# Three more chunks whose activations come already turned round, normalised by GpSimd

## The chip, the cores and the metric

The kernel runs on one core of a Trainium2 chip. A core has five engines that run side by side and meet only at semaphores: TensorE (PE in the profile; its weight loads are PEld), VectorE (DVE), ScalarE (ACT), GpSimd (POOL) and SyncE (SP), which here does nothing but start DMA transfers. ACT and POOL also start some. The transfers of all queues share 16 DMA engines. Each engine executes its instructions in the order in which the program lists them, so an instruction that waits holds up all that stand behind it on that engine or queue.

The metric is device time in microseconds (us) for one execution: 358.87 before the change, the median of three runs (358.83 to 359.21).

## The reference

Two branches work on the same normalised rows, and their results are added to the input. S = 2048 rows, D = 448, F = 1792, all float32.

```python
x  = A_q
xn = _layernorm(x)                      # over the 448 columns, no weights
# A: short convolution of k (4 taps), times v, a long causal convolution by FFT, gate
k_shift = sum(k_pad[:, t:t + S] * shift_k[:, ks - 1 - t] for t in range(ks))
kv = k_shift * v
y  = causal_conv(kv, ssm_k) + kv * ssm_D
# B: dense 448 -> 1792, Mish, dense 1792 -> 448
h  = einsum("bsd,df->bsf", xn, w1) + b1
B  = einsum("bsf,fd->bsd", mish(h), w2)
return x + xn * y + B
```

## The kernel before, in words

**Tiling.** The 2048 rows lie as 128 partitions by 16 tiles; two tiles make a chunk of 256 rows, so there are 8 chunks, c = 0 to 7. The dense branch handles one (chunk, pair of 128-wide blocks of F) after another: 8 chunks by 7 pairs, 56 pairs. Pair i takes two slots of the schedule: in slot 2i the first product `g1_mm(i)` (22 matmuls, line 512), in slot 2i+1 the Mish of that pair on ACT (`mish`, line 520, then a split by lines 84 and 85) and the second product `g2_mm(i-2)` of the pair two before (12 matmuls, lines 544 to 546). To keep float32 precision at the fast matmul rate every operand is split into a high part (a rounding copy on ACT) and a low part (a subtraction on DVE): `XH`/`XL` for the activations, `w1h`/`w1l`, `w2h`/`w2l` for the weights, `ach`/`acl` for the Mish results. In g1_mm of a pair of chunk 1 or later the first seven matmuls need only XH; then come four that need XL.

**The long convolution** is an FFT by matmuls, threaded through the same slots. In slots 6 to 59 it transforms 8 groups of the filter (`h`) and 8 of kv: load, `f1_mm` (line 146, 8 matmuls), `f1_fold` (a copy on ACT, line 152, and two DVE operations, line 156, into one of two buffers `st`), and `f1_out`, which stores st to device memory (line 167), from the POOL queue for the two filter groups in slots 6 and 9, from ACT's afterwards. kv is made by `taps` on DVE (lines 189 to 202) and one tap on POOL (`taps_pool`, line 182), for which `skb`, the four rows of shift coefficients repeated on 128 partitions, must be there.

**The order** is written by hand: `at(slot, ...)` puts work ahead of the slot's products, `after(slot, ...)` behind them; within a slot the order is that of the calls. The loop over chunks stands last, so its loads are the last of their slot. Some DVE work is put in a list (`drip`), of which one item is issued at each call `dv()`, that is, behind most DVE operations; a flush empties the list.

**Weights.** During chunk 0 the raw weights arrive pair by pair on SP's queue (w1, w2 in turn) and are split once: `w2_load(4)` in slot 9, `w2_load(5)` in slot 10, `w2_split(4)` at the end of slot 11, `w2_split(5)` at the end of slot 13.

**Normalising, two ways.** The first product needs the activations with D on the partitions. `NT = 4` is the first chunk that uses the second way.

- Chunks 1 to 3 (`ln_stats`, `ln_T`): q is loaded with rows on the partitions; DVE takes mean and variance (lines 406, 409, 412), POOL the power -1/2 (415), subtracts and multiplies (419), copies a tail (423); in the last two slots before the chunk, eight PE transposes (line 464, two sets of four) turn the result, and ACT and DVE split it out of PSUM (476, 474). The transposes need `ident`, a part of the tile `con`.
- Chunks 4 to 7 (`nt_...`): q is loaded the same way for the statistics, and a second copy, already turned by the host, goes to the tile `xn` (`xT_load`, line 434, 512 KB; there is one buffer xn). Mean and factor are stored to device memory (`nt_store`, POOL's queue, line 442, 2 KB) and read back as a row repeated on all partitions (`nt_row`, SP's queue, line 445, 128 KB, one for each half of the chunk) into `idr`, which lies over `ident`. DVE subtracts and multiplies by that row (`nt_norm`, line 451, two operations of 128x512 for a half), ACT and DVE split (`nt_split`, 458, 459).

The slots of the second way are counted from a base b = 14(c-1), plus 1 where the table says so:

```python
NT_AT = {"q": -5, "x": -1, "stats": -2, "flush": 0, "row": (4, 8), "norm": (7, 10), "split": (8, 11)}
```

Of the kernel before, what the change touches and what calls it, by code (L numbers as in the profile page):

```python
# [17 lines left out]
NP = NF // 2  # L18
CH = 256
NCHUNK = S // CH  # L20
NO = 8
EPS = 1e-5

G2_LAG = 2
# [5 lines left out]
I2_AT = {100: ((6, 7, 0, 1), 92, (95, 97, 98, 99), (0, 2, 0, 1)),  # L30
         108: ((2, 3, 4, 5), 101, (104, 105, 106, 107), (0, 1, 0, 1))}
LATE = 2
NT = 4
NT_AT = {"q": -5, "x": -1, "stats": -2, "flush": 0, "row": (4, 8), "norm": (7, 10), "split": (8, 11)}
NT_SOON = dict(NT_AT, row=(4, 5), norm=(4, 7), split=(6, 8))
NT_HOW = {c: NT_SOON for c in (3, 4, 7)}
NT_HOW[5] = dict(NT_AT, q=-8, stats=-4, flush=-2)
WARM_N = (448, 448, 448)
FILL_N = (224, 112, 96)
# [3 lines left out]
def tile_kernel(ctx: ExitStack, tc, q, qT, k, v, sk, hT, sD, w10, w1, w2, c_fib, c_g, c_gi, c_i2, out):  # L43
    nc = tc.nc
    V = nc.vector
# [17 lines left out]
    Dkv = dp.tile([NO * 16, 32, D], F32, name="Dkv")  # L63
    E = dp.tile([NJ * 4, 64, D], F32, name="E")
    MR = {c: dp.tile([2, CH], F32, name="MR") for c in range(NT, NCHUNK)}

    con = cp.tile([128, 64 + CH], F32, name="con")
    f1, ident, idr = con[:, 0:64], con[:, 64:192], con[:, 64:]
# [6 lines left out]
    def rs(c):  # L75
        return rstd[:, 2 * c:2 * c + 2] if c < NT else mv[:, 2 * c:2 * c + 2, 1]

# [26 lines left out]
    def dv(n=1):  # L104
        for _ in range(n):
            if drip:
                drip.pop(0)()
# [4 lines left out]
    def at(slot, fn, *args):  # L112
        plan.setdefault(int(slot), []).append((fn, args))

    def after(slot, fn, *args):
        plan2.setdefault(int(slot), []).append((fn, args))
# [4 lines left out]
    skb = sp1.tile([128, 4, D], F32, name="skb")  # L121
# [273 lines left out]
    def xn_tile():  # L395
        return mp.tile([128, 4, CH], F32, name="xn", bufs=1)

    def ln_parts(c):
        st = mp.tile([128, 2, 6], F32, name="bst", bufs=2)
        ve = mp.tile([128, 2], F32, name="ve", bufs=2)  # L400
        if c < NT:
            XN[c] = xn = xn_tile().rearrange("p a b -> p (a b)").rearrange("p (j d) -> p j d", j=2)
        eng = nc.gpsimd if 0 < c < NCHUNK - 1 else V

        def stats(jj):
            V.bn_stats(st[:, jj], Q[c][:, jj])

        def aggr(jj):
            V.bn_aggr(mv[:, 2 * c + jj], st[:, jj])

        def eps(a, b):
            V.tensor_scalar(ve[:, a:b], mv[:, 2 * c + a:2 * c + b, 1], EPS, None, op0=ALU.add)  # L412

        def power(a, b):
            nc.gpsimd.tensor_tensor(rs(c)[:, a:b], ve[:, a:b], mhalf[:, a:b], op=ALU.pow)  # L415

        def norm(jj):
            j = 2 * c + jj
            eng.tensor_scalar(xn[:, jj, :D], Q[c][:, jj], mv[:, j, 0:1], rs(c)[:, jj:jj + 1],
                              op0=ALU.subtract, op1=ALU.mult)  # L420

        def tail(a, b, copy=eng.tensor_copy):
            copy(xn[:, a:b, D:], xn[:, a:b, D - 64:D])

        return stats, aggr, eps, power, norm, tail, ve
# [15 lines left out]
    def nt_store(c):  # L441
        nc.gpsimd.dma_start(MR[c].rearrange("j (p t) -> p j t", t=2), mv[:, 2 * c:2 * c + 2])

    def nt_row(c, jj):
        nc.sync.dma_start(idr, MR[c][jj].partition_broadcast(128))

    def nt_norm(c, jj):
        x = XN[c][:, :, 128 * jj:128 * jj + 128]
        for t, op in enumerate((ALU.subtract, ALU.mult)):
            m = idr.rearrange("p (a t) -> p t a", t=2)[:, t:t + 1].to_broadcast([128, 4, 128])  # L450
            V.tensor_tensor(x, x, m, op=op)
            dv()

    def nt_split(c, jj):
        if jj == 0:
# [22 lines left out]
    def ln_T(c, jj):  # L478
        if jj == 0:
            dv(len(drip))  # L480
            x_tiles(c)
        p = pg()
        transposes(c, jj, p)
        for lo in range(2):
            x_split(c, jj, p, lo)
# [73 lines left out]
    def mlp_slot(s):  # L559
# [3 lines left out]
        if half == 0:  # L563
            if i < n:
                c, p = pairs[i]
                if c + 1 < NT:
                    if p == 0:
# [8 lines left out]
        else:  # L576
            if i < n:
                c, p = pairs[i]
                if p == NP - 2 and c + 1 < NT:
                    ln_T(c + 1, 0)  # L580
# [21 lines left out]
        after(t, f1_fold, g, "h")  # L602
        at(t + (2 if t < 12 else 3), f1_out, Dh, g, "h", nc.gpsimd if t < 12 else nc.scalar)

    at(12, lambda: nc.sync.dma_start(skb, sk.partition_broadcast(128)))
    for g in range(-2, 0):
        at(12, k_load, g)
    for g, t in enumerate(KV_AT):
        d = t - (KV_AT[g - 1] if g else t - 6)
        at(t - d - (3 if g > 1 else 2), k_load, g)  # L610
        at(t - d - 1, v_load, g)
        for u in range(4):
            after(t - (2 if g else 1) - d + d * u / 4, taps, g, u)
        at(t, f1_mm, KV, g, "kv")
        if g + 1 < NO:
            after(t, taps_pool, g + 1, 2)
        after(t, f1_fold, g, "kv")
        at(t + (3 if g < NO - 1 else 2), f1_out, Dkv, g, "kv")

    for p in range(NP):  # L620
        if p >= 3:
            at(max(2 * p - 5, 0), w1_load, p)
        if p == 1 or p > 2:
            at(2 * p - 2, w1_split, p)
        p and at(2 * p + (1 if p < 5 else 0), w2_load, p)
        at(2, w2_split, p) if p == 0 else after(2 * (p + G2_LAG) - 1, w2_split, p)

    at(OCT_AT[0], regroup)
    for o in range(NO):
# [34 lines left out]

    for c in range(NT, NCHUNK):
        at_ = NT_HOW.get(c, NT_AT)
        b = 2 * NP * (c - 1) + (1 if c == NT else 0)
        at(b + at_["q"], ln_load, c)
        at(b + at_["x"], xT_load, c)
        at(b + at_["stats"], nt_stats, c)  # L670
        at(b + at_["flush"], lambda: dv(len(drip)))
        for jj in range(2):
            at(b + at_["row"][jj], nt_row, c, jj)
            after(b + at_["norm"][jj], nt_norm, c, jj)
            after(b + at_["split"][jj], nt_split, c, jj)
# [28 lines left out]
    stats, aggr, eps, power, norm, tail, ve = ln_parts(0)  # L704
# [120 lines left out]
```

## Time and profile before

| | |
|---|---|
| median of three runs | 358.87 us (358.83 to 359.21) |
| the profiled execution | 359.38 us |
| its span, first to last instruction | 357.6 us |
| what lies around the span | 1.78 us |
| granted TensorE clock | 0.998 |
| PE busy | 352.0 us, 98% |
| DVE busy | 269.1 us, 75% |
| ACT busy | 156.8 us, 44% |
| POOL busy | 76.5 us, 21% |

Times in the trace count from the start of the span. A row of the timeline has the start, the time (for several instructions from the first start to the last end), the engine, the line, the operation, what it writes and reads, a count, and in brackets the idle time before it with what ended it. An SPq or ACTq row is the issue of a DMA; its landing is told in the view of the DMAs, whose rows end with the size and the us from issue to landing. Neighbouring instructions of an engine overlap a little, so a chain is best followed from start to start. In the groups of instructions the numbers behind the bar are the total and the mean of one in ns.

In the profiled execution chunk 0's first product begins at 9.22 us and chunk 1's (slot 14) at 43.45 us; that of chunk 2 (slot 28) at 78.71, of chunk 3 (slot 42) at 118.68.

### The profile page before, as it was taken

What the parts mean: (1) busy time and instruction counts of PE and PEld (TensorE: products, weight loads), DVE (VectorE), ACT (ScalarE), POOL (GpSimd) and SP (SyncE); (2) the same over time, 40 slices, a digit from 0 to 9 for tenths busy, and PEclk for the clock granted to TensorE, in tenths of its full rate; (3) what the DMA queues carried; (4) which work ended last, traced back from release to release, by engine and by line L of the source; (5) the groups of instructions that cost most, each with busy time, mean ns of one, the idle gap of its engine ahead of it and who ended that gap; (6) DMA issues with size and microseconds to landing.
All of it is one profiled execution on the core that took longest, in us unless ns stands there. A gap on an engine that the chain in (4) does not pass through costs nothing.

```text
span 357.6 us, 7445 instructions
## 1 busy us (share of the span) xinstructions
PE 352.0 (98%) x3100; PEld 290.2 (81%) x3100; DVE 269.1 (75%) x371; ACT 156.8 (44%) x267; POOL 76.5 (21%) x81
## 2 busy tenths in 40 slices
PE   8999999999999999999999999999999999999995
PEld 2988888888888989889997758767775699979795
DVE  5999568999999899899537757756863933788942
ACT  3976643344241542342333453455445343354480
POOL 2037001920128240213000030011031116040030
PEclk9999999999999999999999999999999999999999
DMA  7999978849586446763869569999994386989176
GB/s 242 353 373 303 408 291 221 242 124 285 145 262 217 148 120 169 222 162 82 250 208 353 203 175 295 241 279 310 284 260 131 81 240 252 408 316 284 32 113 144
DMA packets 30227, 82.48 MB, mean 231 GB/s; under 512 B 3057, under 2 KB 15474, under 8 KB 30194
## 3 DMA queue, kind: packets, MB, share of 16 engines
q1 hardware_dynamic: 21410, 47.03, 39.2%
q0 software_dynamic: 4896, 22.95, 22.8%
q10 hardware_dynamic: 3888, 12.03, 12.4%
q8 instruction: 24, 0.39, 0.5%
q14 instruction: 9, 0.07, 0.1%
HBM read 53.55 MB, written 28.45 MB: 229 GB/s over the span
## 4 chain that ended last, share of the span: by engine, by line
PE 86%; DMA 5%; DVE 3%; issue 3%; POOL 2%; SPq 0%; ACT 0%; ACTq 0%; POOLq 0%
PE pg L512 18%; PE pg L544 12%; PE pg L546 12%; PE pg L545 11%; PE pq L512 7%; PE pp L512 5%; PE pr L512 4%; PE pq L146 3%; DMA Dh<-st 3%; PE pp L235 3%; PE pr L235 3%; PE pp L274 2%; DMA kr<-in_w_dram 2%; PE pq L235 2%; PE pr L274 1%
## 5 line engine op out<-in xcount | busy, mean ns | idle before, releaser
L544 PE MATMUL pg<-w2h,ach 128*128 128x448 f32 x224 | 82.4, 368 | 0.0
L545 PE MATMUL pg<-w2l,ach 128*128 128x448 f32 x224 | 81.3, 363 | 0.2 <-DVE w2l L85 0.2
L546 PE MATMUL pg<-w2h,acl 128*128 128x448 f32 x224 | 81.4, 363 | 0.0
L85 DVE TENSOR_TENSOR acl<-a,ach 128x512 fp32r<-128x512 f32 x56 | 38.9, 695 | 32.1 <-ACT ach L84 32.0
L520 ACT ACTIVATE a<-pg,b1t 128x256 f32<-128x256 f32 x66 | 27.8, 472 | 64.3 <-PE pg L512 57.5
L512 PE MATMUL pg<-XH,w1h 128*128 128x256 f32 x264 | 52.7, 283 | 0.0
L544 PEld LDWEIGHTS pg<-w2h,ach 128*128 128x128 f32 x224 | 41.9, 187 | 10.8 <-issue 6.4
L512 PEld LDWEIGHTS pg<-XH,w1h 128*128 128x128 f32 x264 | 41.3, 188 | 6.8 <-issue 6.3
L545 PEld LDWEIGHTS pg<-w2l,ach 128*128 128x128 f32 x224 | 42.1, 188 | 2.9 <-DVE w2l L85 0.5
L546 PEld LDWEIGHTS pg<-w2h,acl 128*128 128x128 f32 x224 | 42.0, 188 | 2.4
L512 PE MATMUL pg<-XL,w1h 128*128 128x256 f32 x264 | 42.9, 277 | 0.0
L156 DVE TENSOR_TENSOR st<-pq,st 128x896 f32<-128x896 f32 x32 | 34.8, 1089 | 5.7 <-ACT st L152 5.0
L512 PEld LDWEIGHTS pg<-XL,w1h 128*128 128x128 f32 x264 | 35.9, 188 | 0.0
L84 ACT CAST ach<-a 128x512 fp32r<-128x512 f32 x56 | 34.8, 622 | 1.7
L512 PE MATMUL pg<-XH,w1l 128*128 128x256 f32 x198 | 33.5, 278 | 0.0
L182 POOL TENSOR_TENSOR x<-kr,skb 128x896 f32<-128x896 f32 x8 | 17.0, 2126 | 71.8 <-DVE x L181 58.6
L512 PEld LDWEIGHTS pg<-XH,w1l 128*128 128x128 f32 x198 | 27.6, 188 | 0.0
L199 DVE TENSOR_TENSOR x<-x 128x896 f32<-128x896 f32 x24 | 26.4, 1100 | 1.0 <-POOL x L182 0.3
L520 ACT ACTIVATE a<-pq,b1t 128x256 f32<-128x256 f32 x20 | 8.4, 471 | 31.8 <-PE pq L512 31.8
L285 POOL DMA_DIRECT2D E<-qe x14 | 8.7, 629 | 63.0 <-ACT qe L282 63.0
L152 ACT COPY st<-pr 128x896 f32<-128x896 f32 x16 | 14.5, 907 | 14.8 <-PE pr L146 12.4
L415 POOL TENSOR_TENSOR mv<-ve,mhalf 128x2 f32<-128x2 f32 x4 | 3.9, 986 | 62.8 <-DVE ve L412 62.8
(138 smaller groups left out, 612.8 us busy)
## 6 DMA issues: line engine op xcount, KB each, us to landing
Dkv<-st ACTq DMA_DIRECT2D x16, 448.0 KB, 6.0
ah<-Dh SPq DMA_DIRECT2D x8, 896.0 KB, 7.7
av<-Dkv SPq DMA_DIRECT2D x8, 896.0 KB, 8.6
e<-E POOLq DMA_DIRECT2D x8, 896.0 KB, 7.4
E<-qe POOLq DMA_DIRECT2D x14, 448.0 KB, 5.9
kr<-in_k_dram SPq DMA_DIRECT2D x10, 448.0 KB, 7.0
Dh<-st ACTq DMA_DIRECT2D x10, 448.0 KB, 6.3
x<-in_hT_dram SPq DMA_DIRECT2D x8, 448.0 KB, 6.8
```

Of the source, the lines that this page charges most:

```text
L84: nc.scalar.copy(h, raw)
L85: V.tensor_sub(l, raw, h)
L152: nc.scalar.copy(st[:, 1], o)
L156: f(st[:, n], e, st[:, 1])
L182: nc.gpsimd.tensor_mul(o, KR[g - u // 2], skb[:, u:u + 1].to_broadcast([128, 2, D]))
L199: V.tensor_add(KV[g], KV[g], o)
L235: nc.tensor.matmul(p[32 * t:32 * t + 32, r, :D], g[rs, t, c], a[rs, t], start=True, stop=True, tile_position=(64 * r, 32 * t))
L512: nc.tensor.matmul(ps[n], l, r, start=all(m[0] != n for m in seq[:n_]), stop=all(m[0] != n for m in seq[n_ + 1:]))
L520: nc.scalar.activation(a[:, n], ps[n], AF.Mish, bias=b1t[:, 2 * p + n:2 * p + n + 1])
L544: nc.tensor.matmul(ps, ah[:, n, cs], w2h[:, f], start=f == 0, stop=False)
L545: nc.tensor.matmul(ps, ah[:, n, cs], w2l[:, f], start=False, stop=False)
L546: nc.tensor.matmul(ps, al[:, n, cs], w2h[:, f], start=False, stop=f == NF - 1)
```

## The change

`NT` becomes 1, so chunks 1 to 3, too, are loaded turned and lose their transposes. For these three, and not for 4 to 7, the subtraction and multiplication by the row are done by GpSimd. The base b now has the plus 1 for chunks 1 to 4 (before for chunk 4 alone, so chunk 4 keeps its slots). Chunk 1 has slots of its own: load of q in 0, statistics from 6, turned copy in 7, flush and store in 7, both rows in 8, norms behind 9, splits behind 12 and 13. Its second row doesn't go to `idr` but to the first part of `skb`, so both can be under way at once; the load of the shift coefficients into skb moves from slot 12 to slot 14. Chunk 2: q in 10, statistics 13, turned copy 14, flush 15, rows 19 and 20, norms behind 19 and 22, splits behind 21 and 23. Chunk 3: q in 20, statistics 26, flush 27, turned copy 28, rows 33 and 34, norms behind 33 and 36, splits behind 35 and 37. Besides, the store of kv groups 0, 2, 4 and 5 (slots 27, 37, 47, 53) moves to the end of its slot, behind the slot's Mish, and `w2_split(5)` moves from the end of slot 13 to the beginning of slot 12.

```diff
-NT = 4
+NT = 1
-NT_HOW = {c: NT_SOON for c in (3, 4, 7)}
+NT_HOW = {c: NT_SOON for c in (4, 7)}
+NT_HOW[2] = NT_SOON
+NT_HOW[1] = dict(q=-1, x=6, stats=5, flush=6, row=(7, 7), norm=(8, 8), split=(11, 12))
+NT_HOW[3] = dict(NT_SOON, q=-9, stats=-3, flush=-2)
+NORM_POOL = 1, 2, 3
...
+    def row_at(c, jj):
+        return skb[:, 0, :CH] if (c, jj) == (1, 1) else idr
+
     def nt_row(c, jj):
-        nc.sync.dma_start(idr, MR[c][jj].partition_broadcast(128))
+        nc.sync.dma_start(row_at(c, jj), MR[c][jj].partition_broadcast(128))
...
         for t, op in enumerate((ALU.subtract, ALU.mult)):
-            m = idr.rearrange("p (a t) -> p t a", t=2)[:, t:t + 1].to_broadcast([128, 4, 128])
-            V.tensor_tensor(x, x, m, op=op)
-            dv()
+            m = row_at(c, jj).rearrange("p (a t) -> p t a", t=2)[:, t:t + 1].to_broadcast([128, 4, 128])
+            (nc.gpsimd if c in NORM_POOL else V).tensor_tensor(x, x, m, op=op)
+            c in NORM_POOL or dv()
...
-    at(12, lambda: nc.sync.dma_start(skb, sk.partition_broadcast(128)))
+    at(14, lambda: nc.sync.dma_start(skb, sk.partition_broadcast(128)))
...
-        at(t + (3 if g < NO - 1 else 2), f1_out, Dkv, g, "kv")
+        (at if t % 2 else after)(t + (3 if g < NO - 1 else 2), f1_out, Dkv, g, "kv")
...
-        at(2, w2_split, p) if p == 0 else after(2 * (p + G2_LAG) - 1, w2_split, p)
+        if p in (0, 5):
+            at(2 if p == 0 else 12, w2_split, p)
+        else:
+            after(2 * (p + G2_LAG) - 1, w2_split, p)
...
     for c in range(NT, NCHUNK):
         at_ = NT_HOW.get(c, NT_AT)
-        b = 2 * NP * (c - 1) + (1 if c == NT else 0)
+        b = 2 * NP * (c - 1) + (1 if c < 5 else 0)
```

## The prediction

> **What bounds the kernel now.** I read the page's shares of busy time first, then the chain that ended last, then the timeline of each engine around the transposes and in chunk 0.
>
> ```profile
> span 357.6 us, 7445 instructions
> PE 352.0 (98%) x3100; PEld 290.2 (81%) x3100; DVE 269.1 (75%) x371; ACT 156.8 (44%) x267; POOL 76.5 (21%) x81
> ...
> PE 86%; DMA 5%; DVE 3%; issue 3%; POOL 2%; SPq 0%; ACT 0%; ACTq 0%; POOLq 0%
> ```
>
> TensorE works in 98% of the span, and 86% of the chain are its matmuls. So a matmul less is time less, as long as everything the next matmul wants is there; and a transposed activation that comes late is time more, one for one. Both happen in this change, the first six times, the second, I think, in chunk 1.
>
> **Step 1: the transposes go.** The timeline of PE at the end of chunk 0, and at the start of chunk 1:
>
> ```profile
> 34.16 0.60 PE L464 MATMUL pg<-con,xn 128*128 128x128 f32 x4
> 34.51 0.45 PE L544 MATMUL pg<-w2h,ach 128*128 128x448 f32 x1
> 34.80 0.37 PE L545 MATMUL pg<-w2l,ach 128*128 128x448 f32 x1
> 35.00 0.37 PE L546 MATMUL pg<-w2h,acl 128*128 128x448 f32 x1
> ...
> 38.04 0.66 PE L464 MATMUL pg<-con,xn 128*128 128x128 f32 x4
> 38.45 0.60 PE L512 MATMUL pg<-XH,w1h 128*128 128x256 f32 x3
> ...
> 43.45 0.52 PE L512 MATMUL pg<-XH,w1h 128*128 128x256 f32 x3
> ...
> 44.25 0.39 PE L512 MATMUL pg<-XL,w1h 128*128 128x256 f32 x2
> ```
>
> A set of four takes 0.35 us (34.16 to 34.51), and the product behind it starts slowly: its second matmul comes 0.29 after the first instead of 0.20. That is 0.44. A set behind a transform (38.04) takes 0.41, and there the slow start stays. Chunks 1 to 3 have three sets of each kind: 3 x 0.44 + 3 x 0.41 = **2.55 us** off PE. Nothing hides them; ACT and DVE split XH and XL as before, only out of SBUF.
>
> **Step 2: chunk 1's row, up to its landing.** Before, the statistics of chunk 1 ran in one piece ahead of a fold; now they are dripped between its two parts, so the fold's time comes first.
>
> ```profile
> 22.70 1.15 DVE L406 BATCH_NORM_STATS2 bst<-qt 128x6 f32<-128x448 f32 x2
> ...
> 24.10 0.17 DVE L412 TENSOR_SCALAR ve<-mv 128x2 f32<-128x2 f32 x1
> 24.18 2.21 DVE L156 TENSOR_TENSOR st<-pq,st 128x896 f32<-128x896 f32 x2
> ...
> 24.36 0.72 POOL L415 TENSOR_TENSOR rstd<-ve,mhalf 128x2 f32<-128x2 f32 x1 [5.54 <-DVE ve L412]
> ...
> 130.64 0.83 POOL L442 DMA_DIRECT2D MR<-mv  x1 [0.29 <-POOL mv L415]
> ```
>
> The statistics end at 24.27 + 2.21 = 26.5; power (0.09 later, 0.72) to 27.3; the store starts 0.29 later, at 27.6. What a store, a row and two weight loads took to land:
>
> ```profile
> MR<-mv POOLq DMA_DIRECT2D x1, 2.0 KB, 3.6
> MR<-mv POOLq DMA_DIRECT2D x1, 2.0 KB, 4.2
> MR<-mv POOLq DMA_DIRECT2D x1, 2.0 KB, 6.6
> con<-MR SPq DMA_DIRECT2D x1, 128.0 KB, 3.9
> kr<-in_w_dram SPq DMA_DIRECT2D x1, 448.0 KB, 5.1
> x<-in_w_dram SPq DMA_DIRECT2D x1, 448.0 KB, 5.8
> ```
>
> No store of the trace falls into chunk 0, so its price is bounded by 3.6 and 6.6. I take 3.6: the 6.6 was chunk 7's, which stood behind two other stores on POOL's queue, and here that queue is empty. The store lands at 31.2, both rows are issued then, and the first lands 3.9 later, at 35.1.
>
> **Step 3: what queues behind the row on SP.** In slot 8 SP now waits for that store. Behind it stand w2(4) and w2(5), the loads of the next slots:
>
> ```profile
> 22.73 0.60 SPq L360 DMA_DIRECT2D kr<-in_w_dram  x1
> ...
> 28.02 0.33 SPq L379 DMA_DIRECT2D kr<-in_w_dram  x1
> ```
>
> Before, SP had issued w1(6) at 22.73 and w2(4) at 28.02, w2(5) 0.38 later. Now the turned copy of chunk 1 (512 KB) goes out at 23.4, the rows from 31.2 to 32.0, w2(4) at 32.0, w2(5) at 32.4: four us later. With 5.1 and 5.8 us they land at 37.1 and 38.2. The other loads of those slots (q, filter group 4, k) move by as much and are wanted many slots later; I cost them at nothing.
>
> **Step 4: from w2(5) to chunk 1's product.** w2_split(4) and (5) now stand ahead of a fold, both splits of chunk 1 and a Mish. The durations, from ACT, DVE and the groups by form:
>
> ```profile
> 41.69 0.91 ACT L152 COPY st<-pr 128x896 f32<-128x896 f32 x1 [2.37 <-DMA Dh<-st]
> 42.49 0.84 ACT L520 ACTIVATE a<-pg,b1t 128x256 f32<-128x256 f32 x2
> 43.37 0.62 ACT L84 CAST ach<-a 128x512 fp32r<-128x512 f32 x1
> 43.89 0.94 ACT L84 CAST w2h<-x 128x896 fp32r<-128x896 f32 x1
> ...
> 44.76 0.68 DVE L85 TENSOR_TENSOR acl<-a,ach 128x512 fp32r<-128x512 f32 x1
> 45.36 1.08 DVE L85 TENSOR_TENSOR w2l<-x,w2h 128x896 fp32r<-128x896 f32 x1
> ...
> L459 DVE TENSOR_TENSOR XL<-xn,XH 128x512 fp32r<-128x512 f32 x8 | 5.5, 689 | 3.2 <-ACT XH L458 3.1
> ...
> L458 ACT CAST XH<-xn 128x512 fp32r<-128x512 f32 x8 | 5.0, 626 | 9.0 <-DVE xn L451 9.0
> ```
>
> ACT from 38.2: w2h(5) 0.94, fold copy 0.91, XH of the first half 0.63, Mish 0.84, cast 0.62, XH of the second half 0.63: 4.57, less about 0.1 of overlap at each of five joints (41.69 + 0.91 ends 0.11 after 42.49): 42.7. DVE follows from 39.15: w2l(5) 1.08, the fold 2.21, XL 0.69, acl 0.68, one of chunk 2's statistics 0.58 (dripped there), XL 0.69: 5.93, less about 0.4: **44.7**. PE wants XH at 43.45 - 0.85 = 42.6 (two sets of transposes less) and XL 0.80 later, at 43.4. It waits **1.3 us**. Had w2(5) come at once, the Mish would lead, which waits for the product of slot 12 (a g2 of 2.4 us ahead of 42.6): from 40.4 over Mish and cast to 41.85, then acl, statistics and XL (0.68 + 0.58 + 0.69) to 43.75: a wait of 0.35 us would stay.
>
> **Step 5: GpSimd's subtraction and multiplication.** Four operations of 512 elements a partition per chunk. No such form is in the trace; the nearest are
>
> ```profile
> L182 POOL TENSOR_TENSOR x<-kr,skb x8: 2118/2128/2134, 61.0 to 162.5; 128x896 f32<-128x896 f32 x8
> ...
> L419 POOL TENSOR_SCALAR xn<-qt,mv,rstd x6: 1872/2662/3605, 25.2 to 112.4; 128x448 f32<-128x448 f32 x6
> ...
> 64.06 2.77 POOL L419 TENSOR_SCALAR xn<-qt,mv,rstd 128x448 f32<-128x448 f32 x1
> 64.07 1.10 DVE L199 TENSOR_TENSOR x<-x 128x896 f32<-128x896 f32 x1
> ```
>
> By the two-input row 2.128 x 512/896 = 1.22 us each, 4.9 for chunk 1: from 35.1 to 40.0, ahead of ACT. The upper end: the other POOL operation stretches by 3605/1872 = 1.93 when others work beside it; then 9.4 us, to 44.5. I take 1.22, the same kind of operation, whose eight instances lie within 16 ns. In chunks 2 and 3 the splits come five slots and more ahead of the product: nothing. The old norms of these chunks (six of 2.66 by the median) go from the same engine.
>
> The Trainium skill (SBUF — State Buffer, SBUF: two separate sides) says that a DVE operation with two SBUF inputs and a GpSimd operation that reads SBUF exclude each other for a whole instruction. The row at 64.07 disagrees: a DVE addition of two SBUF tensors took 1.10 us inside a GpSimd operation that began 0.01 earlier and ran for 2.77. The rule is a rival below.
>
> **Step 6: what else moves.** skb is loaded when GpSimd has finished with chunk 1's second row, at about 40:
>
> ```profile
> skb<-in_sk_dram SPq DMA_DIRECT2D x1, 896.0 KB, 10.1
> ...
> 54.81 1.08 DVE L189 TENSOR_TENSOR x<-kr,skb 128x896 f32<-128x896 f32 x1
> ...
> Dh<-st POOLq DMA_DIRECT2D x6, 448.0 KB, 9.5
> ```
>
> It lands near 50, used first at 54.81: hidden, and only a landing five us later would cost. The store of filter group 3 now stands behind the norms on POOL, issued near 40 and 41, landed near 50; its buffer is wanted by the copy of slot 16, at about that time, and the Mish behind that copy has three slots to spare. The kv stores at the end of their slot free their buffer one Mish and cast (1.5 us) later, with ten slots until it is reused: nothing. Chunk 2's first norm stands ahead of a kv tap on POOL; between a row that has long landed and one that comes late lie 0 and, with 9.5 us for it, some 1.5 us at slot 24. I take 0.
>
> **Sum.** -2.55 + 1.3 = -1.2 us against the profiled execution's 359.38 (span 357.6 and 1.78 around it), so 358.2 for one like it; it stood 0.5 above the median of 358.87, for which I forecast **357.7**.
>
> **The rivals.**
> - *The store lands late, and SP's queue decides (slower).* With 6.6 instead of 3.6 everything from step 2 on is 3.0 later; w2(4) then already holds the product of slot 13. The wait is 4.3, the sum +1.8: **360.7**. It turns the sign once the store takes longer than 4.85 us. For it: chunk 0 is where the loads are thickest, two weight loads took over five us each. Against: the queue holds nothing else, and SP, while it waits, puts nothing on the DMA engines.
> - *Everything arrives.* While SP waits, its transfers drain, so w2(5) may land in 4.6 us: 37.0, the wait is 0.35 at most, the sum -2.2: **356.7**.
> - *GpSimd stretched by 1.93.* Norms until 44.5, XH to 45.1, XL to 45.8: a wait of 2.4, the sum -0.15: **358.7**.
> - *The gain is met at kv, not made.* At the last kv group PE has no slack:
>
> ```profile
> 169.12 0.13 PEld L146 LDWEIGHTS pq<-x,con 32*64 32x64 f32 x2 [0.17 <-DVE x L202]
> ```
>
> DVE ends the product kv just as PE comes to it. If DVE doesn't get earlier too, nothing is gained: **358.9**. Against it: chunk 2's statistics (1.6 us, 24.27 - 22.70) leave that stretch, which is more than the 1.2 us by which PE is early.
> - *The two engines exclude each other.* Then w2l(4) and w2l(5) each wait for one of GpSimd's operations, 1.22 twice, XL comes 2.4 later, the sum is +1.2: **360.1**. The 64.07 row speaks against it. That is the rule from the Trainium skill's page SBUF — State Buffer (SBUF: two separate sides), which the trace doesn't bear out.
>
> **How the numbers follow.** My forecast 0.35, everything arrives 0.15: faster by over 0.2% (0.72 us, about what a measurement of this kernel can tell from no change) 0.50. GpSimd stretched 0.09, kv 0.08: within 0.2%, 0.17. Late store 0.28, exclusion 0.05: slower 0.33. The range goes from just below 356.7 to just above 360.7, 356.4 to 361.0; what it leaves out is a store still later, or the tap of step 6 on top. The likeliest case alone, with a store of 3.6 to 4.2 and weights up to 0.6 faster, has 357.1 to 358.3.
>
> **What would show it.** Right: eight instances of L464 left, all ahead of 10 us; w2(4) issued on SP near 32 behind a wait for MR; ACT waiting for w2's DMA in slots 11 and 12; PE idle 1 to 1.5 us at the start of chunk 1 with ACT's XH or DVE's XL named; no PE wait at chunks 2 and 3. Wrong: a store landing after 32.5 us, GpSimd operations longer than 1.5 us, or idle time of PE at kv transforms.

## The result and the profile after

The change makes the kernel slower: 370.23 us (median of four runs, 370.16 without the first) against 359.04 us of the kernel before on the same chip, a ratio of 1.029 (95% interval 1.027 to 1.032). On the chip of the first experiments it took 367.35 us (366.67 to 368.06) against 359.04: 1.0234 (1.0216 to 1.0252). The execution profiled with the first result took 1974 us, with PE busy for 1967.7 us of it, and is left out of the ratio; the profile read here is that of the same, unchanged kernel in the experiments (label e0_after, 367.75 us for the profiled execution, span 366.0). Everything below is about this second pair, 8.3 us apart; where the first chip lost 2.9 more, no trace shows.

The line numbers have moved, by 4 in the first part of the code and by 7 from the row's load on. L519 is the first product (512 before), L551 to L553 the second (544 to 546), L458 subtraction and multiplication (451), L465 and L466 the splits XH and XL (458, 459), L88 and L89 the splits w2h/ach and w2l/acl (84, 85), L150 the transform (146), L203 and L206 the last steps of taps (199, 202).

The page: the span and engines, the granted clock in 40 slices of 9.15 us, and the chain by engine.

```profile
span 366.0 us, 7421 instructions
PE 353.1 (96%) x3076; PEld 289.8 (79%) x3076; DVE 274.1 (75%) x371; ACT 157.2 (43%) x267; POOL 78.5 (21%) x84
...
PEclk9999789999999999999999999999999999999999
...
PE 68%; DVE 17%; DMA 6%; issue 4%; POOL 2%; ACT 2%; SPq 0%; DVEq 0%; POOLq 0%
```

The 24 transposes are gone (3100 matmuls before, 3076 now), yet PE is busy 1.1 us longer and idle 7.3 us more. Its share of the chain fell from 86% to 68%, DVE's rose from 3% to 17%. The clock, full nearly everywhere, has a dip in slices 5 and 6. Two things have come in, then: something around 40 us that touches PE's clock, and DVE as the bound elsewhere. PE's waits say the same (total us, times, longest):

```profile
PE pg L551 <- ACT w2h L88: 3.1, 1, 3.1
PE pq L150 <- DVE x L206: 1.3, 2, 1.0
PE pq L150 <- DVE st L160: 1.0, 1, 1.0
...
PE pg L552 <- DVE w2l L89: 0.8, 1, 0.8
...
PE pg L519 <- DVE XL L466: 0.2, 1, 0.2
```

**First place: the end of chunk 0.** The chain that ended last (start, us, what), and SP's timeline:

```profile
27.75 6.62 DMA MR<-mv
...
35.38 6.72 DMA kr<-in_w_dram
42.12 0.95 ACT w2h L88
```

```profile
23.52 0.66 SPq L438 DMA_DIRECT2D xn<-in_qT_dram  x1
34.43 0.33 SPq L452 DMA_DIRECT2D con<-MR  x1
...
35.38 0.38 SPq L383 DMA_DIRECT2D kr<-in_w_dram  x1
35.81 0.42 SPq L383 DMA_DIRECT2D x<-in_w_dram  x1
```

The store of 2 KB starts at 27.75, as foreseen, and takes 6.6 us. SP issues nothing from 24.2 to 34.4. w2(4), issued at 28.02 before, goes out at 35.38 and lands 6.7 later, at 42.1; w2(5) takes 7.4. PE, which wants w2(4) for the product of slot 13 at 40.0, stands:

```profile
39.71 0.28 PE L519 MATMUL pg<-XL,w1h 128*128 128x256 f32 x1
43.11 0.74 PE L551 MATMUL pg<-w2h,ach 128*128 128x448 f32 x1 [3.13 <-ACT w2h L88]
44.65 0.74 PE L552 MATMUL pg<-w2l,ach 128*128 128x448 f32 x1 [0.81 <-DVE w2l L89]
...
45.94 0.57 PE L552 MATMUL pg<-w2l,ach 128*128 128x448 f32 x1
46.31 0.57 PE L553 MATMUL pg<-w2h,acl 128*128 128x448 f32 x1
...
48.92 0.52 PE L519 MATMUL pg<-XH,w1h 128*128 128x256 f32 x3
```

Behind the wait the matmuls start 0.37 us apart (45.94 to 46.31) instead of 0.20. The windows show why. Their columns are the window, its us, the busy us of PE, PEld, DVE, ACT and POOL with counts, the granted clock, the DMA engines' share, and GB/s:

```profile
39.00:42.00 3.00, 0.98 (x9) 0.78 (x7) 0.00 (x0) 0.00 (x0) 2.92 (x3) 1.00 0.94 350
42.00:45.00 3.00, 1.08 (x2) 0.64 (x3) 1.91 (x2) 2.67 (x4) 2.77 (x4) 0.51 1.03 417
45.00:48.00 3.00, 3.00 (x9) 2.65 (x9) 2.97 (x4) 2.40 (x6) 0.00 (x0) 0.50 1.03 407
48.00:51.00 3.00, 2.79 (x18) 2.47 (x17) 2.97 (x8) 0.00 (x0) 0.00 (x0) 0.85 1.00 413
```

The granted clock falls to 0.5 for some six us. The wait is paid about 1.6 times: 3.13 + 0.81 + 0.21 = 4.15 us of standing, and the product of slot 13 takes 48.92 - 43.11 - 0.81 = 5.0 us of work where 2.4 are usual, 2.6 more: 6.8 us together.

The same columns for the 6.62 us of this store and, in the kernel before, for the 3.60 us of the store from which step 2 took its price, the one issued at 130.64:

```profile
27.75:34.37 6.62, 6.62 (x55) 5.72 (x55) 6.28 (x9) 4.46 (x8) 1.96 (x3) 1.00 0.91 260
...
130.64:134.24 3.60, 3.60 (x27) 3.48 (x26) 3.53 (x6) 1.51 (x4) 2.96 (x2) 1.00 0.02 1
```

The cheap store had the DMA engines to itself (share 0.02), this one met engines that were busy (0.91).

**Second place: the kv transforms of chunks 1 to 3.** How far PE is behind the kernel before is read from the weight loads of the same transform, at slots 16 and 59. First the two of before, then the two of after:

```profile
48.91 0.13 PEld L146 LDWEIGHTS pq<-x,con 32*64 32x64 f32 x2 [0.31 <-DMA x<-in_v_dram]
...
169.12 0.13 PEld L146 LDWEIGHTS pq<-x,con 32*64 32x64 f32 x2 [0.17 <-DVE x L202]
```

```profile
54.44 0.13 PEld L150 LDWEIGHTS pq<-x,con 32*64 32x64 f32 x2 [0.31 <-issue]
...
176.62 0.13 PEld L150 LDWEIGHTS pq<-x,con 32*64 32x64 f32 x2 [0.17 <-DVE x L206]
```

PE is 5.53 us behind at slot 16 and 7.50 at slot 59. In between, four sets of transposes fewer should bring it 1.70 nearer; so 3.7 us are lost in that stretch. (From there PE stays 7.50 behind to its last product; the last 0.9 of the span's 8.4 come after it.) GpSimd and DVE there:

```profile
72.06 3.68 POOL L458 TENSOR_TENSOR xn<-xn,con 128x512 f32<-128x512 f32 x2 [2.42 <-DMA con<-MR]
```

```profile
64.64 1.74 DVE L89 TENSOR_TENSOR acl<-a,ach 128x512 fp32r<-128x512 f32 x1
...
69.68 1.09 DVE L203 TENSOR_TENSOR x<-x 128x896 f32<-128x896 f32 x1
70.69 0.69 DVE L89 TENSOR_TENSOR acl<-a,ach 128x512 fp32r<-128x512 f32 x1
...
72.49 2.08 DVE L203 TENSOR_TENSOR x<-x 128x896 f32<-128x896 f32 x1
74.60 2.09 DVE L206 TENSOR_TENSOR x<-x 128x896 f32<-128x896 f32 x1
```

The same addition takes 1.09 us alone and 2.08 beside GpSimd's pair (72.06 to 75.74), the same split 0.69 and 1.74. These DVE operations get about 1.0 longer at 896 elements and at 512 alike. A slower rate would take more from the longer one; this looks like a turn waited out. The first place bears it out:

```profile
43.09 1.51 DVE L89 TENSOR_TENSOR w2l<-kr,w2h 128x896 fp32r<-128x896 f32 x1 [6.92 <-ACT w2h L88]
```

This split starts while GpSimd's last operation for chunk 1 is running (its pair goes from 41.01 to 43.65). It ends at 44.60, and its usual 1.08 us counted back from there begin at 43.52, about when GpSimd ends. And the addition at 63.59, which began 0.19 us before GpSimd's pair at 63.78, took its usual 1.09.

### The profile page after: what moved, and what is told of

Read it like the earlier page. It is cut to its first block, busy times and chain, and to the rows that moved or that the text cites. A ratio compares the mean times of both kernels' runs of the same rounds, so it can differ in the third digit from the quotient of the medians.

```text
span 1972.4 us, 7421 instructions
## 1 busy us (share of the span) xinstructions
PE 1967.7 (100%) x3076; PEld 1470.9 (75%) x3076; DVE 277.1 (14%) x371; ACT 158.2 (8%) x267; POOL 75.3 (4%) x84
## 4 chain that ended last, share of the span: by engine, by line
PE 100%; DVE 0%; issue 0%
PE pg L519 25%; PE pg L551 13%; PE pg L552 13%; PE pg L553 13%; PE pq L519 8%; PE pp L519 5%; PE pr L519 4%; PE pq L150 4%; PE pp L239 3%; PE pr L239 3%; PE pp L278 2%; PE pq L239 2%; PE pr L278 1%; PE pp L332 1%; PE pg L699 1%; PE pq L332 0%
## 5 line engine op out<-in xcount | busy, mean ns | idle before, releaser
L551 PE MATMUL pg<-w2h,ach 128*128 128x448 f32 x224 | 345.4, 1542 | 0.0
L553 PE MATMUL pg<-w2h,acl 128*128 128x448 f32 x224 | 345.2, 1541 | 0.0
L552 PE MATMUL pg<-w2l,ach 128*128 128x448 f32 x224 | 342.1, 1527 | 0.0
L551 PEld LDWEIGHTS pg<-w2h,ach 128*128 128x128 f32 x224 | 200.7, 896 | 99.1 <-issue 98.9
L519 PEld LDWEIGHTS pg<-XH,w1h 128*128 128x128 f32 x264 | 210.6, 923 | 54.6 <-issue 54.6
L552 PEld LDWEIGHTS pg<-w2l,ach 128*128 128x128 f32 x224 | 209.9, 937 | 41.0 <-issue 41.0
L553 PEld LDWEIGHTS pg<-w2h,acl 128*128 128x128 f32 x224 | 201.5, 900 | 52.1 <-issue 52.1
L519 PE MATMUL pg<-XH,w1h 128*128 128x256 f32 x264 | 223.6, 1037 | 0.0
L519 PE MATMUL pg<-XL,w1h 128*128 128x256 f32 x264 | 202.3, 1022 | 0.0
L519 PEld LDWEIGHTS pg<-XL,w1h 128*128 128x128 f32 x264 | 197.3, 945 | 0.0
L89 DVE TENSOR_TENSOR acl<-a,ach 128x512 fp32r<-128x512 f32 x56 | 38.7, 692 | 1002.1 <-ACT ach L88 1002.1
L519 PE MATMUL pg<-XH,w1l 128*128 128x256 f32 x198 | 156.1, 1034 | 0.0
L519 PEld LDWEIGHTS pg<-XH,w1l 128*128 128x128 f32 x198 | 150.4, 939 | 0.0
L519 PEld LDWEIGHTS pq<-XH,w1h 128*128 128x128 f32 x80 | 63.7, 936 | 29.4 <-issue 29.4
L150 PE MATMUL pq<-x,con 32*64 32x448 f32 x128 | 75.7, 2527 | 0.0
L150 PE MATMUL pr<-x,con 32*64 32x448 f32 x128 | 75.5, 2521 | 0.0
L519 PE MATMUL pq<-XH,w1h 128*128 128x256 f32 x80 | 68.6, 1054 | 0.0
L519 PE MATMUL pq<-XL,w1h 128*128 128x256 f32 x80 | 59.7, 1021 | 0.0
L519 PEld LDWEIGHTS pq<-XL,w1h 128*128 128x128 f32 x80 | 59.0, 954 | 0.0
L519 PEld LDWEIGHTS pp<-XH,w1h 128*128 128x128 f32 x56 | 43.7, 913 | 15.7 <-issue 15.7
```

The source lines that it names most:

```text
L89: V.tensor_sub(l, raw, h)
L150: nc.tensor.matmul(ps[h][64 * jj:64 * jj + 64, b, :D], f1[rg:rg + 32], x[rg:rg + 32, jj], start=True, stop=True, tile_position=(rg, 64 * jj))
L519: nc.tensor.matmul(ps[n], l, r, start=all(m[0] != n for m in seq[:n_]), stop=all(m[0] != n for m in seq[n_ + 1:]))
L551: nc.tensor.matmul(ps, ah[:, n, cs], w2h[:, f], start=f == 0, stop=False)
L552: nc.tensor.matmul(ps, ah[:, n, cs], w2l[:, f], start=False, stop=False)
L553: nc.tensor.matmul(ps, al[:, n, cs], w2h[:, f], start=False, stop=f == NF - 1)
```

## The experiments

Two theories of the cause stood at the start, and a third, that the clock makes most of it. One: SP's queue is all, and w2(4) behind the store makes the whole loss. The other: GpSimd's twelve operations take time from DVE as well. Later a further cause came up. The edits are against the changed kernel; beside each run stand runs of the kernel before on the same chip (358.7 to 359.0 us).

**e0_after: the changed kernel itself**, for its profile above.

> The changed kernel itself, for a profile in which TensorE runs at full clock. Measured so far: about 370 us, 11 us more than before, so with 2.55 us of transposes gone TensorE must lose 13 to 14 us somewhere. Theory A (SP's queue): the rows wait in slot 8 for the store of chunk 1's mean and factor, w2(4) and w2(5) stand behind them; TensorE waits once, between slots 11 and 14 (36 to 60 us), over 10 us, and SP's wait for the store is over 10 us. Theory B (GpSimd): the wait is where XH of chunk 1 waits for GpSimd's operations, each over 2.5 us instead of 1.22, and there is more of it at chunks 2 and 3 or at kv transforms. Theory C (clock): less than 8 us of it is waiting, the rest is a granted clock under 1 in the stages behind a wait.

367.35 us, ratio 1.0234 (1.0216 to 1.0252). No theory came out whole: SP's wait for the store is 10 us (24.2 to 34.4), but PE's longest is 3.13, not over 10; GpSimd's operations take up to 2.06, not over 2.5, yet PE does wait at kv transforms.

**e1_chunks23: chunk 1 keeps its transposes.**

```diff
-NT = 1
+NT = 2
```

> Chunk 1 keeps its transposes, chunks 2 and 3 lose them; the rest of the change stays. Theory A: the loss is chunk 1's alone; four sets of transposes less give 359.0 - 1.7 = 357.3, and TensorE has no wait over 0.5 us in chunk 0 or 1. Theory B: chunks 2 and 3 carry their share, at least 3 us: 361 or more. Theory C: with no wait at chunk 1 the clock is as before, 357.3.

362.98 us, ratio 1.0114 (1.0095 to 1.0134). Chunk 1's store, rows and the late w2(4) are gone, and the kernel is still 4 us slower than before, although four sets of transposes fewer are worth 1.7. The queue is not all. GpSimd and DVE in this run:

```profile
58.74 3.60 POOL L458 TENSOR_TENSOR xn<-xn,con 128x512 f32<-128x512 f32 x2 [11.11 <-DMA Dh<-st]
```

```profile
59.09 2.08 DVE L203 TENSOR_TENSOR x<-x 128x896 f32<-128x896 f32 x1
61.09 1.79 DVE L89 TENSOR_TENSOR acl<-a,ach 128x512 fp32r<-128x512 f32 x1
...
65.15 1.09 DVE L203 TENSOR_TENSOR x<-x 128x896 f32<-128x896 f32 x1
...
102.22 2.21 DVE L160 TENSOR_TENSOR st<-pq,st 128x896 f32<-128x896 f32 x2
```

The last row is a fold: each of its two operations has one input in SBUF and one in PSUM (pq). GpSimd's next pair runs beside it, from 102.44 to 105.13, and the fold takes the 2.21 us of before.

**e5_chunks23_no_norm: as e1, without GpSimd's eight operations** (rows are still loaded, q goes on unnormalised).

```diff
-NT = 1
+NT = 2
...
     def nt_norm(c, jj):
+        if c in NORM_POOL:
+            return
```

> Chunks 2 and 3 turned, chunk 1 as before, and GpSimd's subtraction and multiplication left out (chunks 2 and 3 stay unnormalised): its eight operations are gone, the rows are loaded all the same. Beside the run with them (363.0). Theory D: DVE's longest two-input operations fall back from 2.1 to 1.1 us, DVE's busy time falls by 5 us, and the time to 359.5 or less. Rival E (the loads of k, late behind SP's new waits, make the loss): DVE still waits for k, and the time stays at 362 or more.

357.85 us, ratio 0.9971 (0.9959 to 0.9982): 5.1 less than e1 for eight operations of an engine that is busy a fifth of the time. DVE's busy time falls from 275.2 to 267.7 us. At slot 59 PE is ahead of before by what four sets of transposes are worth, 169.12 - 167.42 = 1.70, and still so at its last product (351.89 against 353.59); of this, 1.07 shows in the medians.

```profile
167.42 0.13 PEld L150 LDWEIGHTS pq<-x,con 32*64 32x64 f32 x2 [0.15 <-DVE x L206]
```

**e8_one_input: as e1, but each GpSimd operation has one input instead of two.** They are as many, on the same tile and in the same place of the program; they multiply by 1. As they read no row, they wait for none and run 5 to 11 us earlier than in e1.

```diff
-NT = 1
+NT = 2
...
-            (nc.gpsimd if c in NORM_POOL else V).tensor_tensor(x, x, m, op=op)
-            c in NORM_POOL or dv()
+            if c in NORM_POOL:
+                nc.gpsimd.tensor_scalar(x, x, 1.0, None, op0=ALU.mult)
+            else:
+                V.tensor_tensor(x, x, m, op=op)
+                dv()
```

> Chunks 2 and 3 turned, chunk 1 as before, as in the run that took 363.0; but each of GpSimd's eight operations is a multiplication of the same 128x512 elements by the number 1, with one input instead of two (chunks 2 and 3 stay unnormalised). Lock by two inputs: only a GpSimd operation with two tensor inputs holds DVE up for long; DVE's two-input operations stay at 1.1 to 1.5 us and the time is that without the operations, 357.5 to 359. Lock by any reader: DVE's operations take 2.1 us beside them as well, 361 or more.

358.9 us (358.54 to 361.37), ratio 1.001 (0.9994 to 1.0026): 4.1 less than e1 and 1.0 more than e5. The operations are no shorter, but DVE loses far less beside them:

```profile
62.12 3.76 POOL L459 TENSOR_SCALAR xn<-xn 128x512 f32<-128x512 f32 x2
```

```profile
63.45 1.08 DVE L203 TENSOR_TENSOR x<-x 128x896 f32<-128x896 f32 x1
64.55 1.00 DVE L89 TENSOR_TENSOR acl<-a,ach 128x512 fp32r<-128x512 f32 x1
...
91.48 1.49 DVE L203 TENSOR_TENSOR x<-x 128x896 f32<-128x896 f32 x1 [0.28 <-POOL x L186]
```

The addition takes 1.08 us inside the pair of GpSimd operations (2.08 in e1), the split 1.00 instead of 0.69; the longest addition, beside the pair from 91.41, takes 1.49. DVE is busy for 269.8 us, 2.1 more than without the operations, where e1 has 7.5 more. So most of the loss comes not from GpSimd working beside DVE, but from its doing so with two inputs in SBUF. One input still costs some DVE operations 0.3 to 0.4 us; why, these runs don't show.

**e9_no_norm: the change without its twelve GpSimd operations** (all three chunks, rows still loaded).

```diff
     def nt_norm(c, jj):
+        if c in NORM_POOL:
+            return
```

> The change with GpSimd's twelve operations left out (chunks 1 to 3 stay unnormalised), the rows and SP's wait for the store as in the change. Theory D, queue plus exclusion: what stays is chunk 1's wait behind w2(4) and w2(5) with the half clock behind it: TensorE still waits 3 to 4 us near 40, the kv part is as fast as before, 356.4 + 6.8 = 363. If the queue's part was really GpSimd's, 358 or less.

363.6 us, ratio 1.0135 (1.0121 to 1.0149): 3.75 less than the changed kernel, like the 3.7 read above from its trace. What is left is chunk 1's path, where the longest wait of PE stands as it was:

```profile
PE pg L553 <- ACT w2h L88: 3.3, 1, 3.3
```

**e4_row_free: chunk 1's rows are read from an input of the same size**, so SP waits for no store; GpSimd works with these other numbers.

```diff
-        nc.sync.dma_start(row_at(c, jj), MR[c][jj].partition_broadcast(128))
+        nc.sync.dma_start(row_at(c, jj), (sk[jj, :CH] if c == 1 else MR[c][jj]).partition_broadcast(128))
```

> The change, but chunk 1's two rows are read from an input that is always there, not from the stored mean and factor (chunk 1 is normalised by wrong numbers; the same operations run). SP's wait in slot 8 is gone, w2(4) leaves at about 28 again. Theory A (the store behind which SP's queue stands is all of the loss): filter group 4's transform, 5.5 us late in the change, is 0.9 to 1.3 us early, and the time is 357 to 358. Theory D (store and queue cost some 6.8 us at chunk 1, and besides DVE, which bounds slots 20 to 60, is slowed by GpSimd's operations: its two-input additions take 2.08 us instead of 1.09 beside them): group 4's transform is early as well, but 4 us are lost again by the kv transforms, as with chunks 2 and 3 alone: 361 to 363.

363.51 us, ratio 1.0132 (1.0108 to 1.0155): 3.8 less than the changed kernel, with w2(4) issued at 27.64. That is above both theories' figures, and at slot 16 PE is still 2.65 us behind the kernel before (51.56 against 48.91), where it was expected early. No more came of it because chunk 1's GpSimd operations, now at 30.9 to 37.9 us, fall beside weight splits and lengthen these (0.95 to 2.07, 0.42 to 1.44, 0.61 to 1.59 in the rows below), until PE waits 2.2 us for the last:

```profile
33.27 2.07 DVE L374 TENSOR_TENSOR w1l<-kr,w1h 128x768 fp32r<-128x768 f32 x1
35.35 1.44 DVE L375 TENSOR_TENSOR w1h<-kr,w1h 64x256 fp32r<-64x256 f32 x1
36.83 1.59 DVE L605 TENSOR_TENSOR x<-x 1x448 f32<-1x448 f32 x1
```

**e10_row_free_no_norm: both causes away**, the edits of e4 and e9 together.

```diff
     def nt_norm(c, jj):
+        if c in NORM_POOL:
+            return
...
-        nc.sync.dma_start(row_at(c, jj), MR[c][jj].partition_broadcast(128))
+        nc.sync.dma_start(row_at(c, jj), (sk[jj, :CH] if c == 1 else MR[c][jj]).partition_broadcast(128))
```

> Both suspected causes away: the twelve operations left out and chunk 1's rows read from an input that is always there. Theory D: what is left is the change without its costs, 358.9 - 2.55 = 356.4, within 0.5; TensorE's clock full, no PE wait over 0.6 us. If it is over 357.5 a third cause is open.

360.47 us (358.79 to 363.87), ratio 1.0052 (1.0022 to 1.0081): 3.1 less than e9, and 4 more than two causes allow. Something else takes the place of SP's wait. w2(4) and w2(5) go out at 27.64 and 28.02, as before the change, but take 9.1 and 11.9 us to land (5.1 and 5.8 before), and ACT, which has w2_split(5) ahead of the splits of chunk 1, passes the delay on:

```profile
24.00:28.00 4.00, 4.00 (x38) 3.78 (x41) 3.96 (x9) 2.51 (x3) 1.60 (x2) 1.00 1.01 379
28.00:32.00 4.00, 4.00 (x34) 3.14 (x35) 3.21 (x5) 3.94 (x6) 1.45 (x3) 1.00 0.99 319
```

```profile
39.98 0.94 ACT L88 CAST w2h<-x 128x896 fp32r<-128x896 f32 x1 [2.23 <-DMA x<-in_w_dram]
```

The DMA engines are full in this stretch (share 1.01 and 0.99). They were nearly so before the change (0.99 and 0.86 in the same windows); the turned copy of 512 KB and the two rows come on top, ahead of w2(4) and w2(5).

**e12_w2_split_later: e10, and w2_split(5) behind the products of slot 14**, out of the way of chunk 1's splits.

```diff
-        if p in (0, 5):
-            at(2 if p == 0 else 12, w2_split, p)
+        if p == 0:
+            at(2, w2_split, p)
+        elif p == 5:
+            after(14, w2_split, p)
```

> As the run with both causes away (no GpSimd operations for chunks 1 to 3, chunk 1's rows from an input that is always there), which was expected at 356.4 and took 360.5, from 358.8 to 363.9; there w2(5) took 11.9 us to land and ACT and DVE waited for it in front of chunk 1's splits. Here w2_split(5) stands behind slot 14, behind those splits. Theory F (third cause: the split of w2(5), moved to slot 12, makes ACT and DVE wait for a load that the added traffic delays): TensorE's waits at chunk 1 go, 356.4 to 357.3 with little spread. If it stays at 359 or more, the splits wait for the turned copy or something else.

359.46 us (358.28 to 362.86), ratio 1.0034 (1.001 to 1.0058). 1.0 less than e10, but the two ranges overlap widely, so that the gain isn't shown, and theory F's 357.3 was missed: w2(4) still took 11.0 us.

**e13_no_rows: e12, and chunk 1's rows aren't loaded at all.**

```diff
     def nt_row(c, jj):
+        if c == 1:
+            return
```

> As the run before it (no GpSimd operations for chunks 1 to 3, w2_split(5) behind slot 14), and chunk 1's two rows aren't loaded at all. That run took 359.5, its w2(4) still landed 11 us after its issue, and in the trace the rows' 1 KB packets keep the DMA engines busy at 0.9 with 260 to 320 GB/s around 30 us. Theory G (what is left at chunk 1 is the rows' own traffic in front of w2): w2(4) lands in 5 to 7 us, TensorE doesn't wait at chunk 1, 356.4 to 357.3. If it stays at 359 or more, it is the turned copy's 512 KB, or something that these runs don't show.

358.02 us (356.67 to 359.75), ratio 0.9973 (0.9958 to 0.9988). w2(4) landed after 7.1 us, and PE's waits of this stretch are down to 0.3. The profiled execution, 356.67, was the fastest, within 0.4 of what the transposes alone would give (358.9 - 2.55 = 356.3); the median is 1.7 above that, and no trace of such a slower execution was kept. Two repeated rows, 0.26 of the 2.8 MB that moved from 24 to 32 us in e10, so cost some 1.4 us there by what they delay. The rest may lie in the turned copy, which was not tried alone.

**e2_dve_norm: DVE normalises instead of GpSimd.**

```diff
-NORM_POOL = 1, 2, 3
+NORM_POOL = ()
```

> The change, but DVE instead of GpSimd subtracts and multiplies for chunks 1 to 3. Theory A: the queue is what it was, 368 to 371. Theory B: chunk 1's four operations take 0.69 us each on DVE, and 5 us or more come back: under 365; chunks 2 and 3 may lose some at kv.

369.81 us, ratio 1.0298 (1.0283 to 1.0314). No help: DVE now stands 4.68 us before chunk 1's row, the splits of w1, filter and w2 wait behind it, and PE for them:

```profile
38.12 1.42 DVE L458 TENSOR_TENSOR xn<-xn,con 128x512 f32<-128x512 f32 x2 [4.68 <-DMA con<-MR]
```

```profile
PE pq L150 <- DVE x L605: 7.3, 1, 7.3
```

**e3_row_behind: the rows are issued three slots later, behind w2(4) and w2(5)**, the norms two slots later.

```diff
-NT_HOW[1] = dict(q=-1, x=6, stats=5, flush=6, row=(7, 7), norm=(8, 8), split=(11, 12))
+NT_HOW[1] = dict(q=-1, x=6, stats=5, flush=6, row=(10, 10), norm=(10, 10), split=(11, 12))
```

> The change, with chunk 1's rows in slot 11 instead of 8, behind w2(4) and w2(5) on SP, and the norms behind slot 11. Theory A: w2(4) and w2(5) go out near 28 as before the change, and only the row is late: most of the loss comes back, 362 or less. Theory B: the norms come as late or later, 370 or more.

368.89 us, ratio 1.0299 (1.0263 to 1.0335); the expectation fell. w2(4) goes out at 28.12, but the rows can't come before the store has landed (they go out at 34.55 and 34.92), the second took 8.6 us more, and PE waits 6.6 us for the activations XH instead.

**e6_stats_early: chunk 1's statistics and store three slots earlier.**

```diff
-NT_HOW[1] = dict(q=-1, x=6, stats=5, flush=6, row=(7, 7), norm=(8, 8), split=(11, 12))
+NT_HOW[1] = dict(q=-1, x=6, stats=2, flush=3, row=(7, 7), norm=(8, 8), split=(11, 12))
```

> The change, with chunk 1's statistics from slot 3 and the store in slot 4, so that the store leaves near 20 instead of 27.7 us and the rows find it landed. Theory A: chunk 1's wait goes, 357 to 358. Theory D: the wait goes and the kv part stays, 361 to 363, TensorE's clock full throughout. If the store takes 14 us there, both are wrong on the queue and it stays at 367.

370.94 us, ratio 1.0334 (1.0304 to 1.0363); this expectation fell too. The store goes out at 21.89 and lands 8.4 us later, so SP is free about four us sooner. But the store of filter group 1 stands behind it on POOL (22.79 instead of 17.0), its buffer comes free late, and ACT stands 4.06 us at the copy ahead of the weight split:

```profile
22.79 1.23 POOL L171 DMA_DIRECT2D Dh<-st  x2
```

```profile
33.73 0.91 ACT L156 COPY st<-pr 128x896 f32<-128x896 f32 x1 [4.06 <-DMA Dh<-st]
```

**e11_chunk1_dve: only chunk 1 is turned (2 and 3 keep their transposes), statistics early, its rows behind w2(5), DVE normalises behind slot 11**, in search of a version that keeps a third of the gain.

```diff
-NT = 1
+TURN = 1, 4, 5, 6, 7
...
-NT_HOW[1] = dict(q=-1, x=6, stats=5, flush=6, row=(7, 7), norm=(8, 8), split=(11, 12))
+NT_HOW[1] = dict(q=-1, x=6, stats=2, flush=4, row=(9, 9), norm=(10, 10), split=(11, 12))
...
-NORM_POOL = 1, 2, 3
+NORM_POOL = ()
...
-        return skb[:, 0, :CH] if (c, jj) == (1, 1) else idr
+        return skb[:, jj, :CH] if c == 1 else idr
...
-    for c in range(NT, NCHUNK):
+    for c in TURN:
```

> A version meant to keep what pays: only chunk 1 is turned (2 and 3 with transposes), its statistics start in slot 3 and the store leaves in slot 5 behind the store of filter group 1, its rows follow w2(5) on SP and both go to skb, and DVE normalises behind slot 11, where it had idle time before. Gain at most 0.85 us: 358.1. Theory D: 357.9 to 358.9, if the row lands by 36 us and DVE's four operations of 0.69 us fit into its idle time at 38 to 43 us; 361 or more, with the clock at half for some us, if the row lands later, since DVE then stands still before fold and w2l.

364.51 us (363.25 to 365.72), ratio 1.016 (1.0137 to 1.0182). Its rows took 10.6 us to land, and PE waits 2.6 us for XL and 1.9 for XH. With early statistics or late ones, on GpSimd or on DVE, a row for chunk 1 did not come in time.

**e7_moves_only: four chunks with transposes as before; the other moves stay** (skb, w2_split(5), the kv stores).

```diff
-NT = 1
+NT = 4
```

> Only what the change moves besides: chunks 1 to 3 with transposes as before, the shift coefficients in slot 14, four kv stores behind their slot's Mish, w2_split(5) in slot 12. All theories: within 0.7 us of before, 358.3 to 359.8; if it is 361 or more, a part of the loss has been put down to the wrong cause.

358.81 us against 358.92, ratio 0.9998 (0.9989 to 1.0008). These moves by themselves cost nothing that these runs could tell.

**The account.** The 8.3 us between the changed kernel and before, by what each removal took off in the order in which they were made (medians, from several chips):

| part | from | us |
|---|---|---|
| transposes | step 1 of the prediction; e5 shows 1.70 for two chunks of three | -2.55 |
| GpSimd's operations | e0 less e9 | +3.75 |
| SP's wait for the store, with the halved clock | e9 less e10 | +3.1 |
| w2_split(5) ahead of chunk 1's splits | e10 less e12 (ranges overlap, not shown) | +1.0 |
| two repeated rows among the weight loads | e12 less e13 | +1.4 |
| not settled, perhaps the turned copy in chunk 0 | e13 less 356.3 | +1.7 |
| sum | | +8.4 |

Since every line is a difference between neighbours, the sum can't but come out; it proves no line. In the other order the store's wait takes off 3.8 (e0 less e4) and the operations 3.0 (e4 less e10). The last four lines, 7.2, are chunk 1's path, for which 6.8 were read from the trace. In the changed kernel itself, where w2(4) leaves only after the rows and lands in 6.7 us, SP's wait makes that delay; the last three lines appear once it is gone, when rows, turned copy and weights are under way together. No version that computes everything was found to be faster than the kernel before.

## Why the prediction was wrong

The forecast was 357.7 us, in a range of 356.4 to 361.0. The kernel became slower, by 8.3 us on the chip of the traces and 11.2 on the first, with 367.35 and 370.23. Two steps failed: the store's price in step 2, and in step 5 the cost at nothing of what GpSimd does to DVE.

- **Step 1 was right.** The matmuls are 24 fewer, and 0.85 us a chunk holds: 1.70 for two at slot 59 in e5.
- **Step 2 failed, in one term.** The store starts at 27.75 (27.6 foreseen), but takes 6.6 us, not 3.6. The 3.6 was taken because the 6.6 of before stood behind two other stores on its queue. That reason didn't hold: this one stood behind none, the last before it on that queue having landed by 26 us. In the other runs the store of chunk 1 took 5.8 (e2) to 10.0 us (e12). What goes with the price is the share of the DMA engines. In the trace of before it was 0.02, 0.05 and 0.57 during the stores of 3.6, 4.2 and 3.4 us, and 0.86 during that of 6.6; here it was 0.91, in e12 1.00. No run changed the share alone, so this is read from the traces, not tried.
- **Step 3 had the right mechanism**, with the numbers of step 2: w2(4) at 35.4 instead of 32.0. The loads themselves were priced too low, 6.7 and 7.4 us instead of 5.1 and 5.8.
- **Step 4** looked one slot too late: it priced w2(5) at the product of slot 14, and what stood was the product of slot 13, for w2(4). (Its sum for ACT should be 42.3, not 42.7; nothing hangs on it, since DVE ends later.) With w2(4) at 42.1 the product of slot 13 stands 3.1 and 0.8 us, and chunk 1's XL only 0.2 more. That was the rival "the store lands late", whose wait of 4.3 us compares with 4.15 measured. Its price, +1.8 and 360.7, was still too small: it counted a wait once, and the clock behind it made it 6.8. With 2.5 more it would have been 363.2; e9, which has this cause without GpSimd's operations, took 363.6.
- **Step 5 failed**, by the row on which it rested. GpSimd's operations took 1.28 to 2.06 us, longer than the 1.22 taken and shorter than the upper end of 2.36, and that mattered little; what they did to DVE mattered. The row at 64.07 shows a GpSimd operation with one tensor in SBUF and two numbers per partition; those of the change have two tensors. The Trainium skill (SBUF — State Buffer, SBUF: two separate sides) has the rule that the prediction set aside, and the trace agrees with it for these operations: 2.08 us instead of 1.09 for a DVE addition, and 4.1 us of time between e1 and e8. For GpSimd with one input, which the rule's words take in too, e8 shows no wait for a whole instruction: 1.08 to 1.49 for the addition. The rival "the two engines exclude each other" had the mechanism but looked for it only at w2l(4) and (5) in chunk 0; it fell on the kv work from 63 us on, where step 5 costed chunks 2 and 3 at nothing because their splits come early. They do; it is DVE's other work that pays. The rival was given 0.05.
- **The kv rival** had the place right: DVE has no slack there at the last groups. It foresaw that a gain is not realised there, not that about a microsecond of DVE's time is added for each of GpSimd's operations.
- **Step 6 was right** on the moves by e7, which has no row and no norm of chunks 1 to 3. The tap on POOL behind chunk 2's first norm, which e7 can't show, made DVE wait 0.4 us in all (line 186) against 0.3 before (182).
- **What would show it wrong** named a store landing after 32.5 (34.4), GpSimd operations above 1.5 us (up to 2.06) and idle PE at kv transforms (2.3 us): all three came. As rivals they stood singly, and each alone stayed below 361; together, and with the clock, they left the range.

## What to carry to other kernels

Price a small transfer by rows of the trace that fall where the DMA engines are as full as they will be at the new place, and follow what is queued behind whatever waits for it. Before work is given to an idle engine, look for a row with the same kinds of operands beside the engine that it must not disturb, and ask which stage that engine bounds. A wait of PE of some three us should not be counted once only: here 4.15 us of waits cost 6.8, since the clock fell behind the longest.

## What the runs showed of the hardware

- The granted clock fell to 0.51 and 0.50 in the two windows behind a wait of 3.13 us, and was 0.85 in the next; matmuls that start 0.20 us apart at full clock started 0.37 apart. The Trainium skill (TensorE: Matmul & The Clock Gate, Part 1: The HAM clock gate) has it that an idle window of some 3.4 us halves the clock and a busy one restores it; the wait here was a little shorter, and the half speed lasted some six us.
- A DVE operation with two SBUF inputs that meets a GpSimd operation with two SBUF inputs ended up to about 1.0 us later, at 512, 896 and 448 elements alike (0.69 to 1.74, 1.09 to 2.08, 0.61 to 1.59), and less where GpSimd was about to end (1.08 to 1.51). Eight such GpSimd operations kept DVE busy for 7.5 us more (e1 less e5). The GpSimd operation itself went from 1.28 up to 2.06.
- With one SBUF input on GpSimd's side the same addition took 1.08 to 1.49 us and DVE was busy for 2.1 us more (e8 less e5). A DVE fold with one input in PSUM took 2.21 us beside two-input GpSimd operations, as without them (e1).
- The store of 2 KB took 3.4 to 4.2 us where the share of the DMA engines was 0.02 to 0.57, and 5.8 to 10.0 us in chunk 0 (share 0.91 in the changed kernel, 1.00 in e12). The load of w2(4), 448 KB, took 4.5 us in e5 and 11.0 in e12. Without the two rows of 128 KB it took 7.1 (e13).
